# Channel mixing as 512 and 384 columns, and the last 64 keys' product as native float32

## The chip, the core and the metric

One core of a Trainium2 chip runs the whole program. The metric is the time of one execution on the device, in microseconds. Three runs of the kernel before took 436.41 to 436.9, with a median of 436.66.

## The reference

Three networks in a row, all in float32, on 2 batches of 448 tokens. First attention with 12 heads of 64, whose scores are capped by a tanh; then a gated network that mixes tokens; then a token and a channel mixing:

```python
scores = cap * np.tanh((q @ k.T) / sqrt(64) / cap)
attn = softmax(scores);  x = attn @ v                 # (2, 448, 768)
h = gelu(x @ w_in);  u, v = h[..., :512], h[..., 512:]
v_s = w_sg @ layer_norm(v) * g_ln + b_sg
x = x + (u * v_s) @ w_out
u = x + tokens(np.maximum(x.T @ w_tok1, 0) @ w_tok2)   # w_tok1 448x256
out = u + np.maximum(u @ w_ch1, 0) @ w_ch2             # w_ch1 768x1536
```

The change is in two places: `attn @ v` for the last 64 of the 448 keys, and the last line.

## The kernel before, in words

Activations lie as channels by tokens: 128 channels on the partitions, 448 tokens of one batch along the row. Nearly every product is done in three: an operand is split into a high part, rounded to the fp32r format, and a low part, the rest of it; high by high, high by low and low by high are added up in PSUM (`three`, `THREE`). The high part is a cast, the low part a subtraction, on whichever of ScalarE, VectorE and GpSimd the planner picks (`cast`, `rest`, `split`). Each 448-column product of this kind is one matmul, recorded at L276.

Attention runs over 12 pairs of heads (6 per batch). The 448 keys of a pair are three blocks of 128 and a remainder of 64. For the blocks, scores are fp32r products on 64 rows, one head on the lower and one on the upper half of TensorE (L545), then tanh and exp on ScalarE (L519, L527), then the product with the values in native float32 on 128 rows (L577), the operands unsplit. For the 64 remaining keys the two heads share one product on 128 rows (L660), tanh and exp give `tr`, and `tr` is split into `TH` and `TL`. The values of those keys come with the pair's queries and keys as 128 extra columns (`RC`) of the `qk` tensor, so they are split together with them (L353, L357 or L352, and L369). `rest_of` then adds their part to the two heads' outputs: three terms, each for the lower and the upper head, six fp32r products on 64 rows (L566). Normalising the pair follows on VectorE.

After attention come the gated network, token mixing (`tok1_unit`, `tok2_unit`) and channel mixing. `ch1_unit` makes one of 12 blocks of 128 hidden channels: 18 products of 448 columns for batch 0, 18 for batch 1, then a split ReLU. `ch2_unit` makes one of 6 blocks of output channels: 36 products for batch 0, 36 for batch 1, and adds the residual, which GpSimd sums up from its two parts beforehand (L911), on VectorE (L1031). Each batch has 6 tiles `x` of its own for these inputs, [128, 2, 448].

The order of all this is not that of the code. A planner (`Plan.schedule`) gives each operation a duration, due key and possible engines, and lists it on the engine where it can start first; buffers are handed out by due keys too, from the counts in `BUFS`. The emitted order is what every engine then follows.

Of the kernel before, what the change touches and what calls it, by code (L numbers as in the profile page):

```python
# [17 lines left out]
NP = H // 2  # L18
DM = H * D
ND = DM // 128  # L20
DF = 512
NF = DF // 128
ST = 112
NS = S // ST
NR = 3
# [7 lines left out]
KJ = (0, 576, 704, 832)  # L33
QC, RC = slice(128, 576), slice(960, 1088)
QKW = 1088
THREE = ((0, 0), (0, 1), (1, 0))
# [33 lines left out]
}  # L70
BUFS = {"x": 12, "v": 3, "q": 6, "a": 21, "r": 2, "t": 3, "h": 13, "p": 6, "gm": 4, "sc": 2, "sm": 4}
SLOT = 203.0
# [19 lines left out]


class Op:
    __slots__ = ("ways", "key", "seq", "deps", "bufs", "new", "eng", "fn", "start", "end", "nbytes", "nwait")


class Plan:
# [5 lines left out]
    def op(self, ways, key, r=(), w=(), nbytes=0):  # L104

        o = Op()
        o.ways, o.key, o.seq, o.nbytes = ways, key, len(self.ops), nbytes
        o.deps, o.new = [], []
        o.bufs = list(dict.fromkeys(list(r) + list(w)))
        for b in o.bufs:  # L110
            if b.users == 0 and b.ap is None:
                o.new.append(b)
            b.users += 1
            write = any(b is x for x in w)
            if write or b.psum:
                o.deps += b.last_writers + b.readers
                if write:
                    b.last_writers, b.readers = [o], []
                else:
                    b.readers = [o]  # L120
            else:
                o.deps += b.last_writers
                b.readers.append(o)
        o.deps = list(dict.fromkeys(o.deps))
        self.ops.append(o)
        return o

    def schedule(self):
# [13 lines left out]
        free = {t: [0.0] * n for t, n in BUFS.items()}  # L142
        for b in {b for o in ops for b in o.bufs if b.ap is not None and b.tag in free}:
            free[b.tag].pop()
# [78 lines left out]
class Net:  # L223
    def __init__(self, tc, io, pool, ps, anycap=False):
        self.tc, self.nc, self.io, self.pool, self.ps, self.anycap = tc, tc.nc, io, pool, ps, anycap
        self.plan = Plan()
        self.key = 0.0
        self.last_exp = None
        self.exps = {}
# [11 lines left out]
    def h(self, shape, dtype=F32):  # L241
        return self.buf("h", shape, dtype)

    def bank(self):
# [224 lines left out]
    def pair_in(self, n):  # L469
# [30 lines left out]
        def part(i, rows, cs):  # L500
# [3 lines left out]

        V = self.buf("v", [128, 9, 64])
        self.load(
            128 * 576 * 4,
            lambda: nc.sync.dma_start(out=V.ap.rearrange("p c d -> p (c d)"), in_=io["va"][b, p]),
# [25 lines left out]
    def scores(self, qk, js, key, more=(), extra=0.0):  # L534
# [5 lines left out]
        def fn():  # L540
# [10 lines left out]
        self.pe(  # L551
            3 * len(js) + 3 * len(more) + 0.5,
            fn,
# [5 lines left out]

    def rest_of(self, qk, T, A):  # L560
        part, tiles = qk[:2]
# [6 lines left out]
        return fn, [*tiles, *T], A  # L568

# [17 lines left out]
    def normalise(self, n, A):  # L587
# [30 lines left out]
        for h, rows in ((0, LO), (1, UP)):  # L618
# [9 lines left out]
            )  # L628
        x = self.buf("x", [128, 2, S], F32R)
        self.split(S, lambda: x[:, 0], lambda: x[:, 1], lambda: xf.ap, [xf], [x], kn, ON["XH"], ON["XL"])  # L630
        return x

    def attention_all(self):
# [3 lines left out]
        for n in range(B * NP + 1):  # L637
            k0 = 10.0 * n
            if n < B * NP:
                qk = self.pair_in(n)  # L640
                E = {j: self.a([128, 2, S]) for j in range(3)}
                tr, TH, TL = self.h([128, 1, S]), self.h([128, S], F32R), self.h([128, S], F32R)
                A = [self.bank() for _ in range(2)]
                for js in ([[0], [1]] if n == 0 else [[0, 1]]):
                    for i, (j, sc) in enumerate(zip(js, self.scores(qk, js, k0 + 0.3 * js[0]))):
                        self.weigh(sc, 2, E[j], k0 + 0.1 * j)
            if old:
                oqk, oE, oT, oA = old
                self.values(oqk, oE, oA, [0, 1], k0 + 0.5)
                more = [self.rest_of(oqk, oT, oA)]  # L650
            if n < B * NP:
# [4 lines left out]
                def last(sc=sc, part=qk[0]):  # L656
# [8 lines left out]
                self.rest(  # L665
                    S,
                    lambda TL=TL: TL.ap,
                    lambda tr=tr: tr[:, 0],
                    lambda TH=TH: TH.ap,
                    [tr, TH],  # L670
                    [TL],
                    k0 + 5,
                    ON["TL"],
                )
            else:
                f, r, w = more[0]
                self.pe(3.5, f, r, w, k0 + 4)
            if old:
                self.values(oqk, oE, oA, [2], k0 + 5)
                xs.append(self.normalise(n - 1, oA))  # L680
            if n < B * NP:
                old = qk, E, (TH, TL), A
        return xs

    def attention_anycap(self, n):
# [10 lines left out]
        for h, r in ((0, LO), (1, UP)):  # L696
            for m in range(NS):
# [68 lines left out]
                )  # L766
        x = self.buf("x", [128, 2, S], F32R)
        self.split(S, lambda: x[:, 0], lambda: x[:, 1], lambda: xf.ap, [xf], [x], k0 + 8)
# [213 lines left out]

    def tok2_unit(self, h1, w2, x2, d):
        nc = self.nc
# [7 lines left out]
        self.dve(S, lambda: nc.vector.tensor_tensor(out=z.ap, in0=ps[:, :S], in1=z.ap, op=ALU.add), [ps, z], [z])  # L992
        u = self.buf("x", [128, 2, S], F32R)
        self.split(S, lambda: u[:, 0], lambda: u[:, 1], lambda: z.ap, [z], [u])
# [3 lines left out]
    def ch1_unit(self, ws, U, f):  # L998
        ps = self.bank2()
        for b in range(B):  # L1000
            terms = []
            for d in range(ND):
                n, c = divmod(f % 2 * ND + d, 4)
                cs = slice(c * 128, (c + 1) * 128)
                terms += self.three(
                    lambda i, n=n, cs=cs: ws[n][:, i, cs], lambda i, d=d, b=b: U[b][d][:, i], [ws[n], U[b][d]]
                )
            self.mm(ps, lambda b=b: ps[:, b, :S], terms, 1)
        hi, lo = (self.buf("q" if f < 3 else "a", [128, 2, S], F32R) for _ in range(2))
        self.relu_split(2 * S, (hi, lambda: hi.ap), (lo, lambda: lo.ap), ps, lambda: ps[:, :, :S])  # L1010
        return [[hi, lo]] * B, lambda i, b: (hi, lo)[i][:, b]

    def ch2_unit(self, ws, h2, U, d):
        nc, io = self.nc, self.io
        for b in range(B):
            ps = self.bank()
            terms = []
            for f in range(NC):
                cs = slice(f % 4 * 128, (f % 4 + 1) * 128)
                terms += self.three(  # L1020
                    lambda i, f=f, cs=cs: ws[f // 4][:, i, cs], lambda i, f=f, b=b: h2[f][1](i, b), [ws[f // 4], *h2[f][0][b]]
                )
            self.mm(ps, lambda ps=ps: ps[:, :S], terms, 1)
            u = U[b][d]
            cuts = [slice(0, S // 2), slice(S // 2, S)] if (b, d) == (B - 1, ND - 1) else [slice(0, S)]
            o = [self.h([128, cs.stop - cs.start]) for cs in cuts]
            for i, cs in enumerate(cuts):
                self.whole(o[i], u, cs)
                self.dve(
                    cs.stop - cs.start,  # L1030
                    lambda o=o[i], ps=ps, cs=cs: nc.vector.tensor_tensor(out=o.ap, in0=ps[:, cs], in1=o.ap, op=ALU.add),  # L1031
                    [ps, o[i]],
                    [o[i]],
                )
            for i, (cs, out) in enumerate(zip(cuts, (nc.sync, nc.scalar))):
                self.load(
                    128 * (cs.stop - cs.start) * 4,
                    lambda o=o[i], b=b, cs=cs, out=out: out.dma_start(
                        out=io["out"][b, d * 128 : (d + 1) * 128, cs], in_=o.ap
                    ),  # L1040
                    [],
# [4 lines left out]
    def run(self):  # L1046
# [49 lines left out]
        for b in range(B):  # L1096
            U[b] = stage([lambda d=d: self.tok2_unit(h1[b], w2, x2[b], d) for d in range(ND)], 1.1)

# [40 lines left out]
def layout(q, k, v, cap, moe_w_in, moe_g_ln, moe_w_sg, moe_b_sg, moe_w_out,  # L1139
# [9 lines left out]
    qk = np.zeros((B, NP, 2, 64, QKW), q.dtype)  # L1149
    va = np.ones((B, NP, 128, 9, 64), v.dtype)  # L1150
    qk[..., RC] = 1.0
    for h in range(2):
# [5 lines left out]
        qk[:, :, h, :, QC] = q.reshape(B, NP, 2, S, D)[:, :, h].transpose(0, 1, 3, 2)  # L1158
        qk[:, :, h, :, RC.start + 64 * h : RC.start + 64 * h + 64] = vp[:, :, h, REST]
    return {  # L1160
        "qk": qk.reshape(B, NP, 128, QKW),
        "va": va.reshape(B, NP, 128, 576),
        "q": c(qt),
# [21 lines left out]
def build(arrays):  # L1185
# [6 lines left out]
    }  # L1192
    io["out"] = nc.dram_tensor("out_t", (B, DM, S), F32, kind="ExternalOutput").ap()
    with tile.TileContext(nc) as tc:
# [12 lines left out]
```

## Time and profile before

| | us |
|---|---|
| median of three runs | 436.66 |
| the profiled execution's own time | 437.02 |
| its span, first to last instruction | 435.1 |
| TensorE busy (2050 matmuls) | 424.8 |
| VectorE busy | 267.3 |
| ScalarE busy | 248.2 |
| GpSimd busy | 99.8 |

The busy time of an engine is an average over stages. Whether a stage is bound by it is read from the chain of waits, which goes back from the last instruction to what released each step. The granted TensorE clock is 1.00 in nearly all of the span. A native float32 product stands in the trace as two matmul records with a weight load each. A matmul's recorded duration is longer than its step, since products overlap; so steps are taken from starts, or from a run of many.

### The profile page before, as it was taken

The page shows a single profiled execution, that of the slowest core. Times are in us where ns is not written, and L with a number is a line of the kernel's source. Part 1 is how long each engine was busy: PE and PEld are TensorE (multiplying, and loading weights), DVE is VectorE, ACT ScalarE, POOL GpSimd, SP SyncE. Part 2 cuts the span into 40 slices and gives each one's busy share as a digit, 9 for nine tenths or more (in the row PEclk, how much of TensorE's full clock was granted, in tenths as well). Part 3 has the DMA queues.
Part 4 walks back from the last instruction along what each step waited for, and adds up shares of the span by engine and source line. Part 5 has one row for each costly group of instructions (what it writes and reads, how often), then busy time and mean ns, then how long its engine had stood idle before and what let it go on. Part 6 is the DMA issues. An engine that isn't in the chain of part 4 may idle for free.

```text
span 435.1 us, 5461 instructions
## 1 busy us (share of the span) xinstructions
PE 424.8 (98%) x2050; PEld 350.4 (81%) x2050; DVE 267.3 (61%) x422; ACT 248.2 (57%) x375; POOL 99.8 (23%) x100
## 2 busy tenths in 40 slices
PE   8997999999999999999999999999999999999994
PEld 5554556667676899999999999999999999999993
DVE  4799999887559966995567898665113233334210
ACT  5998899886858647527567717766223243253100
POOL 0343351121001321755023681201010011011100
PEclk9999999999999999999999999999999999999999
DMA  7535345464010302105302114544101232533010
GB/s 270 210 127 175 93 147 187 135 213 149 21 51 5 140 2 96 44 0 165 121 0 101 45 50 145 194 134 156 50 0 58 89 124 86 187 124 133 22 44 29
DMA packets 14866, 44.84 MB, mean 103 GB/s; under 512 B 1904, under 2 KB 4208, under 8 KB 14832
## 3 DMA queue, kind: packets, MB, share of 16 engines
q1 hardware_dynamic: 14688, 44.30, 30.5%
q8 instruction: 18, 0.29, 0.3%
q14 instruction: 16, 0.13, 0.1%
q10 hardware_dynamic: 144, 0.11, 0.1%
HBM read 41.65 MB, written 2.75 MB: 102 GB/s over the span
## 4 chain that ended last, share of the span: by engine, by line
PE 90%; DVE 6%; ACT 3%; issue 1%; POOL 0%; DVEq 0%; POOLq 0%
PE gm L276 52%; PE sc L276 21%; PE gm L577 9%; PE sc L545 4%; PE gm L566 1%; DVE t L454 1%; PE sc L660 1%; DVE q L369 1%; ACT a L519 1%; PE sc L925 1%; ACT a L527 1%; DVE t L443 1%; PE sc L344 1%; DVE h L621 1%; DVE h L597 0%
## 5 line engine op out<-in xcount | busy, mean ns | idle before, releaser
L276 PE MATMUL gm<-a,a 128*128 128x448 f32 (+1 forms) x556 | 115.2, 363 | 0.0
L276 PEld LDWEIGHTS gm<-a,a 128*128 128x128 f32 x556 | 102.8, 188 | 8.4
L276 PE MATMUL sc<-x,a 128*128 128x448 f32 x432 | 89.4, 368 | 0.0
L276 PEld LDWEIGHTS sc<-x,a 128*128 128x128 f32 x432 | 81.1, 188 | 8.2
L577 PE MATMUL gm<-a,v 128*128 128x448 f32 x144 | 60.6, 553 | 1.6 <-ACT a L527 1.6
L276 PE MATMUL gm<-q,a 128*128 128x448 f32 x268 | 57.3, 367 | 0.0
L432 DVE SCALAR_TENSOR_TENSOR t<-r,t 128x512 int32<-128x512 int32 (+1 forms) x52 | 39.7, 766 | 28.0 <-ACT t L425 28.0
L412 ACT ACTIVATE t<-r 128x512 uint16<-128x512 uint16 (+1 forms) x52 | 40.8, 784 | 24.8 <-DVE a L369 20.5
L276 PEld LDWEIGHTS gm<-q,a 128*128 128x128 f32 x268 | 50.3, 188 | 4.7
L401 ACT ACTIVATE r<-r 128x512 f32<-128x512 f32 (+1 forms) x58 | 38.9, 671 | 24.8 <-DMA r<-ch_in 22.2
L577 PEld LDWEIGHTS gm<-a,v 128*128 128x128 f32 x144 | 25.7, 189 | 25.2 <-issue 20.0
L370 POOL TENSOR_TENSOR a<-t,a 128x512 fp32r<-128x512 f32 x19 | 25.8, 1359 | 77.7 <-DVE a L353 59.0
L425 ACT ACTIVATE t<-r 128x512 f16<-128x512 f32 (+1 forms) x52 | 40.2, 774 | 0.0
L369 DVE TENSOR_TENSOR a<-t,a 128x512 fp32r<-128x512 f32 x37 | 26.0, 706 | 21.6 <-POOL a L357 20.1
L357 POOL TENSOR_SCALAR a<-t 128x512 fp32r<-128x512 f32 x18 | 11.1, 619 | 119.7 <-PE gm L276 72.0
L519 ACT ACTIVATE a<-sc,qs 128x896 f32<-128x896 f32 x36 | 35.0, 1004 | 5.3 <-PE sc L545 5.3
L527 ACT ACTIVATE a<-a,acap 128x896 f32<-128x896 f32 x36 | 36.5, 1043 | 0.1
L911 POOL TENSOR_TENSOR h<-x 128x448 f32<-128x448 f32 (+1 forms) x25 | 32.9, 1340 | 11.3 <-PE gm L276 6.1
L276 PE MATMUL gm<-x,a 128*128 128x448 f32 x144 | 31.4, 373 | 0.0
L958 DVE SCALAR_TENSOR_TENSOR a<-sc,a 128x896 fp32r<-128x896 f32 x9 | 9.8, 1092 | 34.3 <-ACT a L955 34.3
L276 PEld LDWEIGHTS gm<-x,a 128*128 128x128 f32 x144 | 27.0, 188 | 3.6 <-issue 1.4
L955 ACT ACTIVATE a<-sc 128x896 fp32r<-128x896 f32 x9 | 8.3, 918 | 33.8 <-PE sc L276 33.8
(102 smaller groups left out, 476.5 us busy)
## 6 DMA issues: line engine op xcount, KB each, us to landing
r<-ch_in SPq DMA_DIRECT2D x36, 512.0 KB, 3.3
r<-w_in_in SPq DMA_DIRECT2D x12, 512.0 KB, 4.1
q<-qk_in SPq DMA_DIRECT2D x11, 544.0 KB, 4.7
v<-va_in SPq DMA_DIRECT2D x12, 288.0 KB, 4.0
r<-w_out_in SPq DMA_DIRECT2D x6, 512.0 KB, 3.5
out_t<-h SPq DMA_DIRECT2D x11, 224.0 KB, 2.0
r<-tok_in SPq DMA_DIRECT2D x2, 512.0 KB, 3.4
t<-w_sg_in SPq DMA_DIRECT2D x4, 224.0 KB, 5.8
```

The lines of the kernel that those rows point to most:

```text
L276: self.nc.tensor.matmul(view(), l, rr, start=(i + m == 0), stop=(i + m == n - 1))
L369: "DVE": ("DVE", n / 0.96 + 155, lambda: nc.vector.tensor_tensor(**args()), not psum),
L370: "POOL": ("POOL", n * 2.3 + 60, lambda: nc.gpsimd.tensor_tensor(**args()), True),
L401: lambda: nc.scalar.activation(raw[:, :, 1].bitcast(F32), raw[:, :, 1].bitcast(F32), AF.Copy, scale=2.0**-112),
L412: lambda: nc.scalar.activation(t.ap.bitcast(U16)[:, 0::2], raw.ap.rearrange("p n t -> p (n t)").bitcast(U16)[:, 1::4], AF.Copy, scale=2.0* ...
L425: lambda: nc.scalar.activation(t.ap.bitcast(F16)[:, 1::2], raw[:, :, 1].bitcast(F32), AF.Copy),
L432: lambda: nc.vector.scalar_tensor_tensor(out=t.ap, in0=raw[:, :, 1], scalar=3, in1=t.ap, op0=ALU.logical_shift_left, op1=ALU.bitwise_or),
L519: lambda: nc.scalar.activation(te.ap, sc[:, 0:nn, :S], AF.Tanh, scale=self.qs),
L527: lambda: nc.scalar.activation(te.ap, te.ap, AF.Exp, scale=self.acap),
L545: nc.tensor.matmul(sc[:, h, :S], part(k, rows, ks), part(q, rows, QC), start=(t == 0), stop=(t == 2))
L577: nc.tensor.matmul(A[h][:, :S], V[:, 3 * j + h : 3 * j + h + 2].rearrange("p c d -> p (c d)"), E[j][:, h], start=(j == 0), stop=(j == 2),)
L911: lambda: self.nc.gpsimd.tensor_tensor(out=out.ap, in0=parts(0), in1=parts(1), op=ALU.add),
```

## The change

For the last 64 keys: `tr` is no longer split. `rest_of` now makes two native float32 products on 64 rows, one per head, with the unsplit `E[3]` and with the values' columns moved from `qk` (1088 to 960 columns) to the tensor `va` (576 to 704). The cast `TH` and the subtraction `TL` of each pair go. The planner's duration for `rest_of` grows from 3 to 3.7 slots.

For channel mixing: the two batches' 896 tokens lie side by side in one tile per channel block (`Part` gives each batch its half, and `x` has 6 tiles of double width), and the products run over tokens 0 to 511 and 512 to 895 instead of over the batches. The output tensor is laid out as (768, 896).

```diff
+WIDE = slice(0, 512), slice(512, 2 * S)
-QC, RC = slice(128, 576), slice(960, 1088)
-QKW = 1088
+QC = slice(128, 576)
+QKW = 960
-BUFS = {"x": 12, "v": 3, "q": 6, "a": 21, ...
+BUFS = {"x": 6, "v": 3, "q": 6, "a": 21, ...
+class Part(Buf):
+    def __init__(self, whole, cs):
+        self.whole, self.cs, self.tag, self.psum = whole, cs, None, False
...
+    @property
+    def ap(self):
+        return self.whole.ap[:, :, self.cs]
...
+    def x_part(self, d, b):
+        if b == 0:
+            self.both[d] = self.buf("x", [128, 2, B * S], F32R)
+        return Part(self.both[d], slice(b * S, (b + 1) * S))
...
-        V = self.buf("v", [128, 9, 64])
+        V = self.buf("v", [128, 11, 64])
...
-            for v, e in THREE:
-                for h, rows in enumerate((LO, UP)):
-                    self.nc.tensor.matmul(A[h][:, :S], part(v, rows, RC), T[e][rows], start=False, stop=False)
+            for h, rows in enumerate((LO, UP)):
+                self.nc.tensor.matmul(
+                    A[h][:, :S],
+                    qk[2][rows, 9:11].rearrange("p c d -> p (c d)"),
+                    E[3][rows, 0],
+                    start=False,
+                    stop=False,
+                )
...
-                self.weigh(sc, 1, tr, k0 + 4.1)
-                self.cast(S, lambda TH=TH: TH.ap, lambda tr=tr: tr[:, 0], [tr], [TH], k0 + 5, ON["TH"])
-                self.rest(
...
+                self.weigh(sc, 1, E[3], k0 + 4.1)
...
     def ch1_unit(self, ws, U, f):
         ps = self.bank2()
-        for b in range(B):
+        for m, ts in enumerate(WIDE):
...
-                    lambda i, n=n, cs=cs: ws[n][:, i, cs], lambda i, d=d, b=b: U[b][d][:, i], [ws[n], U[b][d]]
-                )
-            self.mm(ps, lambda b=b: ps[:, b, :S], terms, 1)
+                    lambda i, n=n, cs=cs: ws[n][:, i, cs],
+                    lambda i, d=d, ts=ts: U[0][d].whole[:, i, ts],
+                    [ws[n], U[0][d], U[1][d]],
+                )
+            size = ts.stop - ts.start
+            self.mm(ps, lambda m=m, size=size: ps[:, m, :size], terms, size / S)
...
     def ch2_unit(self, ws, h2, U, d):
-        for b in range(B):
+        for m, ts in enumerate(WIDE):
...
-            self.mm(ps, lambda ps=ps: ps[:, :S], terms, 1)
+            self.mm(ps, lambda ps=ps, size=size: ps[:, :size], terms, size / S)
```

Three places of the order show what moves. The first is TensorE in the second step of the third pair: its third block of scores (`sc_283`), the remainder of the second pair (`gm_228` and `gm_237` are that pair's two heads, `h_263` and `h_273` its `TH` and `TL`, `q_148` and `q_154` the split values), and the last block's values. Before:

```order
L545 MATMUL sc_283<-q_213 128x448 x2
L545 MATMUL sc_283<-q_218,q_213 128x448 x2
L545 MATMUL sc_283<-q_213,q_218 128x448 x2
L566 MATMUL gm_228<-h_263,q_148 128x448
L566 MATMUL gm_237<-h_263,q_148 128x448
L566 MATMUL gm_228<-h_273,q_148 128x448
L566 MATMUL gm_237<-h_273,q_148 128x448
L566 MATMUL gm_228<-h_263,q_154 128x448
L566 MATMUL gm_237<-h_263,q_154 128x448
L577 MATMUL gm_228<-a_222,v_95 128x448
```

Six products stand between the scores and the values. The same place of the change (`sc_268` the scores, `h_229` the unsplit weights, `v_95` the values, L594 is `rest_of`, L694 the remainder's scores, L611 the values):

```order
L574 MATMUL sc_268<-q_186 128x448 x2
L574 MATMUL sc_268<-q_201,q_186 128x448 x2
L574 MATMUL sc_268<-q_186,q_201 128x448 x2
L594 MATMUL gm_225<-h_229,v_95 128x448
L594 MATMUL gm_233<-h_229,v_95 128x448
L694 MATMUL sc_286<-q_186 128x448
L694 MATMUL sc_286<-q_201,q_186 128x448
L694 MATMUL sc_286<-q_186,q_201 128x448
L611 MATMUL gm_225<-a_214,v_95 128x448
```

Two products are left, first one head's and then the other's, and a product on 128 rows follows them. The second place is TensorE's entry to channel mixing. Before (`sc_2426` and `sc_2483` are the first two units, `x_2302` to `x_2372` the six tiles of batch 0, `x_2382` to `x_2435` those of batch 1):

```order
L276 MATMUL sc_2426<-x_2372,a_2185 128x448 x3
L276 MATMUL sc_2426<-x_2382,a_2165 128x448 x3
L276 MATMUL sc_2426<-x_2405,a_2165 128x448 x3
L276 MATMUL sc_2426<-x_2410,a_2165 128x448 x3
L276 MATMUL sc_2426<-x_2420,a_2165 128x448 x3
L276 MATMUL sc_2426<-x_2424,a_2185 128x448 x3
L276 MATMUL sc_2426<-x_2435,a_2185 128x448 x3
L276 MATMUL sc_2483<-x_2302,a_2185 128x448 x3
```

Batch 1 is first read after 18 products. In the change `x_2200` to `x_2263` are the six tiles of both batches, `sc_2313` and `sc_2335` the first two units:

```order
L305 MATMUL sc_2313<-x_2200,a_2063 128x512 x3
L305 MATMUL sc_2313<-x_2215,a_2063 128x512 x3
L305 MATMUL sc_2313<-x_2227,a_2063 128x512 x3
L305 MATMUL sc_2313<-x_2238,a_2063 128x512 x3
L305 MATMUL sc_2335<-x_2200,a_2083 128x512 x3
L305 MATMUL sc_2335<-x_2215,a_2083 128x512 x3
L305 MATMUL sc_2335<-x_2227,a_2108 128x512 x3
L305 MATMUL sc_2335<-x_2238,a_2108 128x512 x3
L305 MATMUL sc_2313<-x_2251,a_2083 128x512 x3
L305 MATMUL sc_2313<-x_2263,a_2083 128x512 x3
L305 MATMUL sc_2313<-x_2200,a_2063 128x384 x3
```

Twelve products of the second unit have moved ahead of the first unit's last two tiles. The third place is VectorE just before it (L369 and L992 before, L398 and L1015 after): the sums with the residual, and the splits' low parts. Before, the end of batch 1:

```order
L992 TENSOR_TENSOR h_1885<-gm_2374,h_1885 128x448
L992 TENSOR_TENSOR h_1901<-gm_2386,h_1901 128x448
L992 TENSOR_TENSOR h_1915<-gm_2397,h_1915 128x448
L992 TENSOR_TENSOR h_1934<-gm_2412,h_1934 128x448
L369 TENSOR_TENSOR x_2405<-h_1861,x_2405 128x448
L369 TENSOR_TENSOR x_2410<-h_1885,x_2410 128x448
L369 TENSOR_TENSOR x_2420<-h_1901,x_2420 128x448
L369 TENSOR_TENSOR x_2424<-h_1915,x_2424 128x448
L369 TENSOR_TENSOR x_2435<-h_1934,x_2435 128x448
```

All sums stand ahead of the last five low parts. The same of the change:

```order
L398 TENSOR_TENSOR x_2215<-h_1764,x_2215 128x448
L398 TENSOR_TENSOR x_2227<-h_1788,x_2227 128x448
L398 TENSOR_TENSOR x_2238<-h_1799,x_2238 128x448
L1015 TENSOR_TENSOR h_1811<-gm_2292,h_1811 128x448
L1015 TENSOR_TENSOR h_1826<-gm_2304,h_1826 128x448
L398 TENSOR_TENSOR x_2251<-h_1811,x_2251 128x448
L398 TENSOR_TENSOR x_2263<-h_1826,x_2263 128x448
```

The last two sums have moved in between the low parts.

## Rows read from the trace of the kernel before

**Rows 1.** The page: busy us of each engine (share of the span).

```profile
PE 424.8 (98%) x2050; PEld 350.4 (81%) x2050; DVE 267.3 (61%) x422; ACT 248.2 (57%) x375; POOL 99.8 (23%) x100
```

**Rows 2.** Chain of waits in order of time: start us, us, what.

```profile
37.80 1.21 DVE q L369
...
39.03 1.10 ACT q L352
...
43.16 0.99 PE gm L577 x2
...
129.15 0.61 PE gm L566 x6
...
130.56 4.51 PE gm L577 x12
...
250.49 89.28 PE sc L276 x432
339.77 89.29 PE gm L276 x432
```

**Rows 3.** Timeline of TensorE, 36 to 46 us: start us, us, engine, line, what.

```profile
37.44 0.48 PE L545 MATMUL sc<-q 64*128 64x448 f32 x2
39.06 0.67 PE L545 MATMUL sc<-q,q 64*128 64x448 f32 x4 [1.14 <-DVE q L369]
...
41.40 0.57 PE L660 MATMUL sc<-q,q 128*128 128x448 f32 x2
43.16 0.99 PE L577 MATMUL gm<-a,v 128*128 128x448 f32 x2 [1.19 <-ACT a L527]
```

**Rows 4.** Timeline of TensorE around one pair's remainder.

```profile
128.99 0.77 PE L566 MATMUL gm<-h,q 64*128 64x448 f32 x6
129.69 0.47 PE L660 MATMUL sc<-q 128*128 128x448 f32 x1
130.00 0.56 PE L660 MATMUL sc<-q,q 128*128 128x448 f32 x2
```

**Rows 5.** Timeline of TensorE by width; then by-form groups (busy us, mean ns).

```profile
149.67 4.24 PE L276 MATMUL gm<-a,p 128*128 128x512 f32 x18
153.75 14.76 PE L276 MATMUL gm<-x,a 128*128 128x448 f32 x72
168.34 18.00 PE L276 MATMUL gm<-q,a 128*128 128x448 f32 x88
...
225.75 9.52 PE L276 MATMUL gm<-a,a 128*128 128x384 f32 x54
...
L276 PE MATMUL gm<-a,a 128*128 128x384 f32 x88 | 16.2, 338 | 0.0
...
L276 PEld LDWEIGHTS sc<-x,a 128*128 128x128 f32 x432 | 81.1, 188 | 8.2
```

**Rows 6.** Groups in the first 45 us (busy us, mean ns), then timelines of VectorE and GpSimd.

```profile
L370 POOL TENSOR_TENSOR h<-h,h 128x448 fp32r<-128x448 f32 x3 | 3.4, 1136 | 2.9 <-ACT h L352 2.9
L352 ACT CAST h<-h 128x448 fp32r<-128x448 f32 x3 | 1.8, 586 | 0.0
L369 DVE TENSOR_TENSOR h<-h,h 128x448 fp32r<-128x448 f32 x1 | 0.6, 618 | 0.0
...
21.63 1.37 DVE L454 SCALAR_TENSOR_TENSOR t<-r,t 128x512 int32<-128x512 int32 x1
24.23 0.69 DVE L454 SCALAR_TENSOR_TENSOR t<-r,t 128x512 int32<-128x512 int32 x1
37.72 1.28 DVE L369 TENSOR_TENSOR q<-q,q 128x1088 fp32r<-128x1088 f32 x1
...
21.33 1.13 POOL L370 TENSOR_TENSOR h<-h,h 128x448 fp32r<-128x448 f32 x1 [0.99 <-ACT h L352]
```

**Rows 7.** Timelines of VectorE and GpSimd at the entry to channel mixing.

```profile
251.07 5.63 DVE L369 TENSOR_TENSOR x<-h,x 128x448 fp32r<-128x448 f32 x5
...
251.76 10.70 POOL L911 TENSOR_TENSOR h<-x 128x448 f32<-128x448 f32 x8 [1.77 <-DVE x L369]
```

More of the change, by code (lines that the diff above doesn't have):

```diff
@@ L109, in op @@
         o.bufs = list(dict.fromkeys(list(r) + list(w)))
-        for b in o.bufs:
-            if b.users == 0 and b.ap is None:
+        held = []
+        for b in list(o.bufs):
+            if isinstance(b, Part):
+                held.append(b.whole)
+            elif b.users == 0 and b.ap is None:
                 o.new.append(b)
@@ L123, in op @@
                 b.readers.append(o)
+        for b in dict.fromkeys(held):
+            if b.users == 0:
+                o.new.append(b)
+            b.users += 1
+            o.bufs.append(b)
         o.deps = list(dict.fromkeys(o.deps))
@@ L142, in schedule @@
         free = {t: [0.0] * n for t, n in BUFS.items()}
-        for b in {b for o in ops for b in o.bufs if b.ap is not None and b.tag in free}:
+        for b in {b for o in ops for b in o.bufs if b.tag in free and b.ap is not None}:
             free[b.tag].pop()
@@ L227, in __init__ @@
         self.key = 0.0
+        self.both = {}
         self.last_exp = None
@@ L551, in scores @@
         self.pe(
-            3 * len(js) + 3 * len(more) + 0.5,
+            3 * len(js) + 3.7 * len(more) + 0.5,
             fn,
@@ L558, in scores, with rest_of @@
         return scs
-    def rest_of(self, qk, T, A):
-        part, tiles = qk[:2]
+    def rest_of(self, qk, E, A):
         def fn():
-            for v, e in THREE:
-                for h, rows in enumerate((LO, UP)):
-                    self.nc.tensor.matmul(A[h][:, :S], part(v, rows, RC), T[e][rows], start=False, stop=False)
-        return fn, [*tiles, *T], A
+            for h, rows in enumerate((LO, UP)):
[6 more added lines that the diff above has]
+                )
+        return fn, [qk[2], E[3]], A
     def values(self, qk, E, A, js, key):
@@ L647, in attention_all @@
             if old:
-                oqk, oE, oT, oA = old
+                oqk, oE, oA = old
                 self.values(oqk, oE, oA, [0, 1], k0 + 0.5)
-                more = [self.rest_of(oqk, oT, oA)]
+                more = [self.rest_of(oqk, oE, oA)]
             if n < B * NP:
@@ L681, in attention_all @@
             if n < B * NP:
-                old = qk, E, (TH, TL), A
+                old = qk, E, A
         return xs
@@ L1035, in ch2_unit @@
             for i, (cs, out) in enumerate(zip(cuts, (nc.sync, nc.scalar))):
+                at = slice(ts.start + cs.start, ts.start + cs.stop)
                 self.load(
[L1037 to L1040, printed above, removed]
+                    128 * size // n * 4,
+                    lambda o=o[i], at=at, out=out: out.dma_start(out=io["out"][d * 128 : (d + 1) * 128, at], in_=o.ap),
                     [],
@@ L1096, in run @@
         for b in range(B):
-            U[b] = stage([lambda d=d: self.tok2_unit(h1[b], w2, x2[b], d) for d in range(ND)], 1.1)
+            U[b] = stage([lambda d=d: self.tok2_unit(b, h1[b], w2, x2[b], d) for d in range(ND)], 1.1)
         c1 = {}
@@ L1149, in layout @@
     qk = np.zeros((B, NP, 2, 64, QKW), q.dtype)
-    va = np.ones((B, NP, 128, 9, 64), v.dtype)
-    qk[..., RC] = 1.0
+    va = np.ones((B, NP, 128, 11, 64), v.dtype)
     for h in range(2):
@@ L1192, in build @@
     }
-    io["out"] = nc.dram_tensor("out_t", (B, DM, S), F32, kind="ExternalOutput").ap()
+    io["out"] = nc.dram_tensor("out_t", (DM, B * S), F32, kind="ExternalOutput").ap()
     with tile.TileContext(nc) as tc:
```

58 lines of the change are left out of this document (30 added, 28 removed).

## Prediction

> **What bounds the kernel now.** I read the page's first block first: TensorE is busy 424.8 of 435.1 us and no other engine above 61% [rows 1]. The chain of waits then says where that matters. Until 43.16 us it runs mainly through VectorE and ScalarE; from there to 429.06 it is TensorE without a gap, and 178.57 us of it are the two channel stages, 864 products in two unbroken pieces [rows 2]. So after 43 us every change of TensorE's time counts in full and relief of another engine counts nothing; before, TensorE waits for VectorE's lateness at two places, which its timeline shows [rows 3]. Third come the steps of single products: in attention [rows 4], and by width [rows 5]. Two tables end the reading: what VectorE, ScalarE and GpSimd do for the last 64 keys in the first 45 us [rows 6], and the entry to channel mixing [rows 7].
>
> **The rest of the keys, product itself.** Removed per pair of heads are six fp32r products on 64 rows. They stand on the chain with 0.61 us [rows 2]: upper and lower half run together, three steps of 0.203. Added are two native products. A native product leaves two records in the trace; twelve records on 128 rows take 4.51 us [rows 2], 0.376 each, so there are four records of 0.376 where six of 0.203 went by twos. No row shows native products on 64 rows. Bounds: two steps, if the heads share as the fp32r ones do (0.75); four, if they share nothing (1.50). The nearest rows are L566's: there the program alternates the halves, and only neighbours in program order run together. In the new code the first head's two records come first and the second head's two behind. In that order record 2 has to wait for record 1 (same rows), record 3 can go beside record 2, record 4 waits for 3: three steps, 1.13 us. I take that: 0.52 more per pair, 12 pairs, +6.2 us (bounds +1.7 and +10.7). What follows each time is a product on 128 rows, so the second head's last record has nothing beside it. In the first pair TensorE still waits for ScalarE, so I take off 0.3.
>
> The Trainium skill (TensorE: Matmul & The Clock Gate, The mechanism) states that products start and end strictly in program order and only weight loads are pulled ahead; it speaks against this part, since by it the cheap bound can't be had. The starts in [rows 4] agree, but show nothing on native records. By it the sum is the one below; were it not so here, the first rival's.
>
> **Around it.** A change between 64 and 128 rows costs some 0.19: from the rest's start to the next product's it is 0.70 instead of 0.61, and that first product takes 0.31 to the next instead of 0.207 [rows 4]. The order has 48 such changes before and 46 after: -0.4.
>
> Removed from the other engines per pair are a cast (0.59 on ScalarE, or on GpSimd) and a subtraction (1.14 on GpSimd, 0.62 on VectorE), and the split of queries and keys shrinks from 1088 to 960 columns (0.15 less of an undisturbed 1.28) [rows 2, 6]. After 43 us all this lies beside TensorE and is worth nothing. Before, it is. At 37.44 TensorE wants the fifth pair's scores and goes on only at 39.06, since VectorE's split of that pair ends at 39.01; at 41.40 it has to wait until 43.16 for ScalarE, which had itself waited for that split until 39.03 [rows 2, 3]. Less the ordinary steps (0.20 and 0.41) these are 1.42 and 1.35, together 2.77 us. Up to there VectorE loses one subtraction (0.6), five smaller splits (0.8) and, where GpSimd's subtraction ran beside it, a stretch (1.37 for an operation of 0.69, while GpSimd's 1.13 ran) [rows 6]. That is 1.4 to 2.1 us; 1.6 is needed, and TensorE itself comes to the place three rests, 1.6 us, later. Both waits should go: -2.8. If they stay or another takes their place, the sum loses what they cost. The queue of loads has the same 832 KB per pair (64 KB go from one tensor to the other) in nearly the same order; I price it at nothing, since the loads before the first scores get shorter, not longer, and from 43 us on no wait for them is on the chain; were one late, ScalarE's wait rather than TensorE's would show it first.
>
> **Channel mixing.** Terms and weights stay; 864 products of 448 columns become 432 of 512 and 432 of 384. In the stages themselves the step at 448 is 89.28 / 432 = 0.2067 [rows 2]. At 512 columns 18 products go from start 149.67 to the next run's at 153.75: 0.2267. At 384 it is 54 in 9.52, from which the last one's own duration of 0.34 comes off: 53 steps of 0.1732 [rows 5]. A pair of 448 costs 0.4133, of 512 and 384 0.3999: 13.4 ns, by 432 gives -5.8 us. The gain is there because 448 lies above the line between its neighbours (0.1999); what does that I can't read. In other stretches 448 runs at 14.59 / 72 = 0.2026 [rows 5]; if the 4 ns belong to the stage and not to the width, the new widths pay them too and the gain falls to 13.4 - 8 = 5.4 ns, -2.3 us. That is the near bound; the far one is nothing at all (third rival). I take -5.8, since both new widths have shown one step throughout. Weight loads of 188 ns [rows 5] did not keep 384 columns from steps of 173.
>
> The price is the entry. So far the first 18 products read batch 0 alone; now the first 512 columns need batch 1 at once. The planner answers by putting the second unit's first twelve products in between: the last two tiles of batch 1 are wanted 24 and 27 products after the start, at +5.4 and +6.1 us, where before it was +6.2 and +6.8. VectorE's last five splits ended at 256.70, 6.2 after the start at 250.49 (5.63 for five, slowed by GpSimd, which added tiles up beside them) [rows 2, 7]. If it does no better, the last tile is some 0.1 late; if the two sums now placed between them cost some 0.4 each there, 0.9; nothing, if GpSimd starts its sums later, as its order says. I take +0.3. A stage 3% shorter asks for its weights 3% sooner; the chain has no gap in either mixing stage now [rows 2], and both preparing engines have time left over the whole span [rows 1], so I price that at nothing; if one weight tile were late it would cost a fraction of its own conversion. The tail's halves shrink from 224 to 192 columns: under 0.1, left out.
>
> **Sum**: +6.2 - 0.3 - 0.4 - 2.8 - 5.8 + 0.3 = -2.8 us. The profiled execution took 437.02 (span 435.1 and 1.9 around it), so 434.2; the median of the runs shown is 0.36 lower, so **433.9**.
>
> **Rivals.** (a) The heads share the native products fully: two steps, +1.7 instead of +6.2. For it: the fp32r halves do, two products per 0.203. Against it: the order of the records. Sum -7.3, **429.4**. (b) They share nothing: four steps of 0.376, a rest of 1.50, +10.7. For it: no native product on 64 rows has been seen to share. Against it: the fp32r halves of the same height and columns do share [rows 4]. The place is the end of every pair, twelve times, all but the first few on the chain and those few in TensorE's own order; from a rest of 1.36 us on (the other terms are -9.0, by 12 is 0.75) the kernel is slower than before. Sum +1.7, **438.4**. (c) Uneven widths bring nothing: a step is a fixed part and a part by column, so 512 and 384 cost what two 448 do. Against it: the three steps of [rows 5] do not lie on a line. Were the excess all the stage's, the mixing would stay at 178.6 and the sum would be +3.0, 439.7. The Trainium skill has this rule (TensorE: Matmul & The Clock Gate, Back-to-back issue gap: in ns, the columns by 2.4 and 2.5 more); by it both pairs take 378 ns, an estimate from that page; the trace has 413 for the pair of 448, so it does not agree at this width. (d) The new order is late somewhere that the old one was not: the entry to mixing by its 0.9, or the first 43 us by their 2.8; forecast or a little above, 434.5 to 437.
>
> **How the numbers follow.** Forecast 0.55, with its own range 432.5 to 435.3 (entry, waits, and a step that differs by stage); (a) 0.16; (b) 0.16; (c) 0.05; (d) 0.08. A measurement of this kernel tells 0.2% (0.9 us) from no change: the three runs lie 0.5 apart. Faster, below 435.8: nearly all of the forecast, (a) and half of (d): 0.71. Slower, above 437.5: (b) mostly and (c): 0.19. The same: 0.10. The range from 429.1 to 438.8 leaves out (c) and about a third of (a) and of (b).
>
> **What would show it.** After: the rest's two products take 1.1 us from their first start to the next product's (0.75 or 1.5 for the rivals), with the first and second head's records overlapping once. The chain turns to TensorE well before 43 us and TensorE waits nowhere over 0.5 us between 30 and 45. The mixing's two stages together last 172.8 instead of 178.6, with steps of 0.227 and 0.173; a step of 0.181 at 384 or 0.231 at 512 would be the stage's share. At the entry TensorE stands still under 1 us. Wrong above all: a rest over 1.36 us.

## The result and the profile after

The changed kernel takes 431.58 us (median of 4, 431.17 to 432.13) against 436.78 for the kernel before on the same chip: ratio 0.9882, 95% interval 0.9865 to 0.9899, or 5.2 us less. The forecast was 433.9. The profiled execution took 431.57 us, span 429.8.

The page of the changed kernel, busy time of each engine, answers to [rows 1]:

```profile
PE 420.9 (98%) x2026; PEld 342.5 (80%) x2026; DVE 259.0 (60%) x417; ACT 244.0 (57%) x366; POOL 87.0 (20%) x90
```

The chain of waits (start us, us, what) answers to [rows 2]:

```profile
40.87 0.75 PE gm L594 x4
...
47.78 1.02 ACT a L548
...
127.61 0.75 PE gm L594 x4
...
129.17 4.51 PE gm L611 x12
...
136.33 65.82 PE gm L305 x316
...
249.27 87.17 PE sc L305 x432
336.45 86.82 PE gm L305 x432
```

Three things are to be seen. The remainder, two native products and four records (L594), takes 0.75 us, two steps of 0.375, where 0.61 stood before. The two mixing stages take 173.99 us instead of 178.57. And between 14.6 us and the last product a single tanh at 47.78 is the chain's only piece on another engine, where before VectorE and ScalarE held it until 43.16.

The chain's piece at the end of attention, before:

```profile
137.56 65.80 PE gm L276 x316
```

| us | before | after | difference |
|---|---|---|---|
| start to the end of attention (start of the piece x316) | 137.56 | 136.33 | -1.23 |
| token stages, with the entry to mixing | 112.93 | 112.94 | 0.0 |
| the two mixing stages | 178.57 | 173.99 | -4.58 |
| last product to the end of the span | 6.1 | 6.5 | +0.4 |

TensorE's timeline (start us, us, engine, line, what) around one remainder answers to [rows 4]:

```profile
82.59 0.47 PE L574 MATMUL sc<-q 64*128 64x448 f32 x2
82.90 0.56 PE L574 MATMUL sc<-q,q 64*128 64x448 f32 x4
83.30 0.91 PE L594 MATMUL gm<-h,v 64*128 64x448 f32 x4
84.14 0.47 PE L694 MATMUL sc<-q 128*128 128x448 f32 x1
84.45 0.57 PE L694 MATMUL sc<-q,q 128*128 128x448 f32 x2
```

From the remainder's first start to the next product's it is 0.84 us, 0.14 more than the 0.70 of before. In the single starts, two records begin 3 ns apart, two more 375 ns later, again 3 ns apart. The same view between 36 and 50 us answers to [rows 3]:

```profile
36.87 0.47 PE L574 MATMUL sc<-q 64*128 64x448 f32 x2
37.18 0.57 PE L574 MATMUL sc<-q,q 64*128 64x448 f32 x4
...
41.86 0.57 PE L694 MATMUL sc<-q,q 128*128 128x448 f32 x2
42.26 4.67 PE L611 MATMUL gm<-a,v 128*128 128x448 f32 x12
...
47.78 0.57 PE L574 MATMUL sc<-q,q 64*128 64x448 f32 x4
48.85 0.47 PE L574 MATMUL sc<-q 64*128 64x448 f32 x2 [0.49 <-ACT a L548]
```

The two waits of before are gone. One is new: from 47.78 to 48.85 are 1.07 us instead of an ordinary 0.41, so 0.66. All twelve records of the values stand ahead of these scores, so three score tiles follow each other, and the third needs the bank that the tanh at 47.78 frees.

In the mixing stages the steps at 512 and 384 columns are 226.7 and 173.3 ns, but not at once. These are the differences of neighbouring starts, in ns, from a change of width on, in one run of each width in the first stage:

```
512: 230 233 236 224 231 236 228 232 231 227 226 227 227 226 227 227 226 227
384: 171 175 177 185 176 182 173 174 173 173 174 173 173 174 173 173 174 173
```

A change to 512 columns costs 41 ns over the even steps, one to 384 costs 26 (4 in one place, where the run of 512 before it had only six products). The 35 changes make 1.13 us, and the first run of 512, behind products of another kind, 0.05 more: nearly the whole distance of 1.19 from 173.99 to the forecast's 172.8.

### The profile page after: what moved, and what is told of

Read it like the earlier page. It is cut to its first block, busy times and chain, and to the rows that moved or that the text cites. A ratio compares the mean times of both kernels' runs of the same rounds, so it can differ in the third digit from the quotient of the medians.

```text
span 429.8 us, 5380 instructions
## 1 busy us (share of the span) xinstructions
PE 420.9 (98%) x2026; PEld 342.5 (80%) x2026; DVE 259.0 (60%) x417; ACT 244.0 (57%) x366; POOL 87.0 (20%) x90
## 4 chain that ended last, share of the span: by engine, by line
PE 96%; ACT 2%; issue 0%; POOL 0%; DVE 0%; DVEq 0%; POOLq 0%
PE gm L305 52%; PE sc L305 20%; PE gm L611 12%; PE sc L574 6%; PE gm L594 2%; PE sc L694 2%; ACT a L548 1%; PE sc L948 1%; PE sc L373 1%; ACT a L556 1%; ACT h L556 0%; ACT r L430 0%; ACT h L548 0%; DVE h L1066 0%; POOL ident masks.py:199 0%
## 5 line engine op out<-in xcount | busy, mean ns | idle before, releaser
L305 PE MATMUL gm<-a,a 128*128 128x384 f32 (+2 forms) x556 | 113.1, 359 | 0.0
L305 PEld LDWEIGHTS gm<-a,a 128*128 128x128 f32 x556 | 100.6, 188 | 8.6
L305 PE MATMUL sc<-x,a 128*128 128x512 f32 (+1 forms) x432 | 87.3, 363 | 0.0
L305 PEld LDWEIGHTS sc<-x,a 128*128 128x128 f32 x432 | 78.3, 188 | 8.9
L611 PE MATMUL gm<-a,v 128*128 128x448 f32 x144 | 59.7, 548 | 0.4 <-ACT a L556 0.4
L305 PE MATMUL gm<-q,a 128*128 128x448 f32 (+2 forms) x268 | 57.0, 366 | 0.0
L399 POOL TENSOR_TENSOR a<-t,a 128x512 fp32r<-128x512 f32 x18 | 24.5, 1362 | 118.7 <-DVE a L382 105.0
L611 PEld LDWEIGHTS gm<-a,v 128*128 128x128 f32 x144 | 26.2, 189 | 22.7 <-issue 19.5
L398 DVE TENSOR_TENSOR a<-t,a 128x512 fp32r<-128x512 f32 x38 | 29.2, 770 | 19.6 <-POOL a L386 18.7
L548 ACT ACTIVATE a<-sc,qs 128x896 f32<-128x896 f32 x36 | 35.0, 1004 | 7.8 <-PE sc L574 7.6
L305 PE MATMUL gm<-a,x 128*128 128x512 f32 x108 | 26.5, 401 | 0.0
```

The lines of the kernel that those rows point to most:

```text
L305: self.nc.tensor.matmul(view(), l, rr, start=(i + m == 0), stop=(i + m == n - 1))
L398: "DVE": ("DVE", n / 0.96 + 155, lambda: nc.vector.tensor_tensor(**args()), not psum),
L399: "POOL": ("POOL", n * 2.3 + 60, lambda: nc.gpsimd.tensor_tensor(**args()), True),
L548: lambda: nc.scalar.activation(te.ap, sc[:, 0:nn, :S], AF.Tanh, scale=self.qs),
L611: nc.tensor.matmul(A[h][:, :S], V[:, 3 * j + h : 3 * j + h + 2].rearrange("p c d -> p (c d)"), E[j][:, h], start=(j == 0), stop=(j == 2),)
```

## The experiments

Theory: (1) the heads share the native products fully, because a record on one half of the rows may pass records that wait for the other half; (2) the lighter VectorE took TensorE's early waits away; (3) mixing gains by width and loses at each change of width. Rivals stand in the expectations. Each run has executions of the kernel before on its own chip beside it; their medians lie between 436.65 and 436.92 us, so times from two different runs are compared to no better than 0.3 us.

**Mixing alone** (mix_alone): the changed kernel with the remainder and its split of before.

```diff
-                    qk[2][rows, 9:11].rearrange("p c d -> p (c d)"),
-                    E[3][rows, 0],
...
+            for v, e in THREE:
+                for h, rows in enumerate((LO, UP)):
+                    self.nc.tensor.matmul(A[h][:, :S], part(v, rows, RC), T[e][rows], start=False, stop=False)
```

> The attention of before (the last keys' product as three fp32r products a head), with only the channel mixing of the change: joined tiles, 512 and 384 columns. If the two parts of the change act apart from each other, the attention ends where it does in before (TensorE's chain up to 137.6 us), the two mixing stages take 174.0 us together as in the changed kernel (178.6 before) and the tail keeps its 0.5 us: some 4.1 us under before. Rival: the gain belongs to the new instruction order as a whole, and the attention moves too: the chain then leaves 137.6 us by over 0.5 us, and the sum with the other part run alone is not the 5.2 us of both together.

432.29 us, ratio to before 0.9897 (0.9882 to 0.9913): 4.4 less. The chain:

```profile
137.41 65.80 PE gm L305 x316
...
250.34 87.17 PE sc L305 x432
337.51 86.82 PE gm L305 x432
```

Attention ends within 0.15 us of before, and the stages are the changed kernel's to 0.01 us. Mixing's gain does not hang on the rest of the change. TensorE's two early waits stand here as before (1.1 us for VectorE, then 1.2 for ScalarE): they hang on the part that is left out.

**The remainder alone** (rest_alone): 448 and 448 columns on the joined tiles.

```diff
-WIDE = slice(0, 512), slice(512, 2 * S)
+WIDE = slice(0, S), slice(S, 2 * S)
```

> The whole change but with 448 and 448 columns in the channel mixing on the joined tiles: the native product and its order alone. By the two-step reading of the trace (1.7 us more products, the 2.8 us of VectorE-caused waits gone, one new wait of 0.7 us): 1.2 us under before, the chain at 136.3 us instead of 137.6, and the mixing stages at 178.6 us with steps of 206.7 ns and no longer steps after a change of tokens. Rival: the longer steps (up to 185 and 236 ns) that the changed kernel shows at the start of each run of one width come from the joined tile and not from the change of width: then some steps of 215 ns stand here too and the stages take 179.8 us.

435.18 us, 0.9964 (0.995 to 0.9978): 1.5 less. The chain, from its first long piece:

```profile
1.63 3.88 DMA cap<-cap_in
...
6.49 2.61 PE sc L574 x12
...
137.06 65.82 PE gm L305 x316
...
250.01 89.28 PE sc L305 x432
339.29 89.29 PE gm L305 x432
```

The stages are as long as before, and every step in them is 206 or 207 ns: the joined tile is not what makes steps longer. The two early waits are gone here, and TensorE's only wait after 10 us is one of 0.5. This profiled execution started its scores late, behind the load of the cap; so the end of attention, 137.06, is not to be compared to 0.5 us, and that this part brings more than 1 us rests on the median. The parts alone make 5.8 us, together 5.2; the intervals, 0.6 to 0.7 us to either side of each, leave that difference open.

**Turned order of widths** (turn_about): 20 changes of width instead of 35 (the expectation counted some 18).

```diff
-        for m, ts in enumerate(WIDE):
+        for m, ts in list(enumerate(WIDE))[:: 1 if f % 2 else -1]:
```

(In the second stage the same with `d`.)

> The changed kernel with the two widths in turned order in every second unit (512, 384, then 384, 512), so that the width changes some 18 times in the two stages instead of 36. If each change of width costs the 35 ns that the eight steps behind it show in the trace of the changed kernel: 0.6 us less, and the stages take 173.4 us instead of 174.0. Rival: the longer steps belong to the start of each group of products into a new bank of PSUM, whatever its width: then every second run still shows them in its middle, and the time is the changed kernel's within 0.2 us.

431.10 us, 0.9872 (0.9857 to 0.9887). The chain:

```profile
249.23 86.87 PE sc L305 x432
336.10 86.62 PE gm L305 x432
```

173.49 us, 0.50 less for 15 changes fewer, 33 ns each. In a run of one width the steps in the middle, where a new bank begins, are no longer than the others. So the extra belongs to the change of width. The medians, 0.48 apart, agree, though the two ranges overlap.

**Heads apart** (heads_apart): the score tiles' products head by head.

```diff
-                for t, (k, q) in enumerate(THREE):
-                    for h, rows in enumerate((LO, UP)):
+                for h, rows in enumerate((LO, UP)):
+                    for t, (k, q) in enumerate(THREE):
```

> The changed kernel with the three products of a score tile issued head by head (three on the lower 64 rows, then three on the upper) and not in turn; 36 such tiles. If TensorE starts its records strictly in the order of the program, only the third of the lower head has the first of the upper beside it: five steps of 0.2 us instead of three, 0.4 us more for each tile, 14 us in all (446 us), wherever TensorE is the bound. If a record on one half of the rows may pass one that waits for the other half, three steps remain and the time is the changed kernel's within 1 us. This tells why the two-record native product of the heads takes two steps: in the second case by passing, in the first because its records already come in turn.

431.96 us, 0.4 over the changed kernel, not 14. TensorE's timeline around the same remainder as above:

```profile
82.89 0.48 PE L574 MATMUL sc<-q 64*128 64x448 f32 x2
83.20 0.57 PE L574 MATMUL sc<-q,q 64*128 64x448 f32 x4
83.60 0.92 PE L594 MATMUL gm<-h,v 64*128 64x448 f32 x4
```

The six products still take 0.71 us. In the starts the upper head's first record begins 10 ns behind the lower's, not behind its third; 10 ns for 36 tiles is 0.36 us; the two ranges of times overlap, so the 0.4 rests on the starts. The compiled program lists the lower head's three products first, as the code does, so the records pass on the chip. The Trainium skill (TensorE: Matmul & The Clock Gate, The mechanism) has matmuls strictly in program order; here the trace does not agree, and the measurement decides.

**Six and six** (heads_far): in eleven pairs the first two tiles' products as six lower, then six upper.

```diff
-            for sc, j in zip(scs, js):
+            for h, rows in enumerate((LO, UP)):
+                for sc, j in zip(scs, js):
...
```

> The changed kernel with the first two score tiles of each of eleven pairs issued as six products on the lower 64 rows, then six on the upper (the other score tiles three and three). If a record may pass any number of records that wait for the other half, these two tiles still take six steps, with the upper head some 20 ns behind the lower: within 0.7 us of the changed kernel. If TensorE can only look past a few, the upper head starts when the lower has that few left, each of the eleven places is longer by at least one step (0.2 us), and the time is over 2 us longer; the step at which the upper head starts tells how far it looks.

437.02 us (one execution), 5.4 over the changed kernel. Its timeline at one such place, and its chain there:

```profile
81.15 0.47 PE L574 MATMUL sc<-q 64*128 64x448 f32 x1
81.46 0.57 PE L574 MATMUL sc<-q,q 64*128 64x448 f32 x2
81.67 0.56 PE L574 MATMUL sc<-q 64*128 64x448 f32 x2
```

```profile
81.22 1.93 PE sc L574 x12
83.15 3.20 PE gm L611 x8
```

1.93 us instead of 1.42. The lower head starts three products alone. The last line is the upper's first product, at 81.67, and the lower's fourth, 0.2 us behind it. When the upper starts, the lower's third has just begun (6 ns earlier) and three still wait; it is so in all eleven places. Passing has a limit. The lower's fourth product carries a wait for its bank, so this run by itself cannot tell a limit of three records from a stop at that wait; the next one can.

**The remainder doubled** (rest_double).

```diff
-            for h, rows in enumerate((LO, UP)):
+            for h, rows in ((0, LO), (0, LO), (1, UP), (1, UP)):
```

> The changed kernel with the last keys' product issued twice for each head, first both of the lower head, then both of the upper: eight records, and the output adds these keys twice. If the upper head's records may pass the four of the lower head that stand before them (nothing among them waits for a semaphore), the eight take four steps of 0.375 us, 1.5 us instead of 0.75 in the chain, and 12 of them add at most 9 us (some 8 to 9 us in all, 439.5 to 440.5). If TensorE starts records strictly in order, only one of the upper's has a lower beside it: seven steps, 2.6 us, 22 us more. If it looks past only three records, five steps: 1.9 us, 13.5 us more.

441.75 us (one execution). The chain and the timeline around one:

```profile
88.45 0.80 PE sc L574 x6
89.25 1.61 PE gm L594 x8
90.86 0.81 PE sc L694 x3
```

```profile
89.09 1.77 PE L594 MATMUL gm<-h,v 64*128 64x448 f32 x8
90.79 0.47 PE L694 MATMUL sc<-q 128*128 128x448 f32 x1
```

Eight records take 1.61 us: four steps and 0.11, not 1.9 or 2.6. The upper head's first record begins 6 ns behind the lower's first, past three that wait; its later ones run 0.11 behind. Twelve times 0.86 more is 10.3; measured, 10.2, a little over the 9 expected, for those 0.11. Native records pass as fp32r ones do. The weight loads show how far. In the changed kernel, where two records of the lower head stand ahead, both heads' first weights are loaded within 10 ns of each other, some 0.2 us before the first record starts. Here, where four stand ahead, only the lower's are; the upper's first load begins 4 ns behind the start of the lower's first record, when three are left waiting. Both hold in eleven of the twelve pairs, where no record among these waits for a semaphore; in the last pair the first load itself waits for one. So three are passed and four are not, and the stop in heads_far needs no wait to explain it.

**The split kept** (split_kept): the two tiles are made as before; nothing reads them.

```diff
+                TH, TL = self.h([128, S], F32R), self.h([128, S], F32R)
...
+                self.cast(S, lambda TH=TH: TH.ap, lambda tr=E[3]: tr[:, 0], [E[3]], [TH], k0 + 5, ON["TH"])
+                self.rest(
...
```

> The changed kernel in which the weights of the last 64 keys are still split into two fp32r tiles by VectorE, GpSimd or ScalarE, as before; nothing reads these tiles. If TensorE's 2.8 us of waits near 37 and 41 us went because this split (and VectorE's share of it) went, waits of over 1 us that end at VectorE come back before 60 us and the time rises by 1 to 2.8 us over the changed kernel's 431.6 (to 432.6 to 434.4). Rival: they went with the narrower q and k tiles or with the new instruction order, and the time stays within 0.4 us.

432.67 us, 1.1 over the changed kernel. TensorE's waits from 14 to 140 us (engine, line waited for: us in total, times, longest; the changed kernel has only the wait for L548 there, once, 0.5 us), then the chain:

```profile
PE sc L574 <- ACT a L548: 1.0, 2, 0.5
PE gm L305 <- DVE h L655: 0.7, 1, 0.7
PE sc L574 <- DVE q L398: 0.2, 1, 0.2
```

```profile
54.53 1.06 DVE q L398
55.59 1.55 DVE t L483
...
60.52 1.14 DVE q L398
61.69 0.63 DVE h L655
...
137.84 65.82 PE gm L305 x316
```

The chain runs through VectorE until after 61 us, and attention ends 1.5 us later, in an execution that was 0.5 over its median. The split's work, with the order that the planner makes for it, is worth 1.1 to 1.5 us, at the low end of what was expected. The sign that was expected did not come: no wait of over 0.7 us came back at one place, the loss is spread.

**Wider tiles** (q_wide): `QKW = 1056` for 960.

> The changed kernel with tiles of 1056 instead of 960 columns for keys and queries (before had 1088): three quarters of the removed columns are loaded and split again, and nothing reads them. VectorE's part of a tile (1.28 us at 1088 columns in before) grows by some 0.11 us and its transfer by a tenth. If the narrower tiles took the two waits away: 1 to 2.8 us over the changed kernel's 431.6. If the split of the last weights did, as predicted: within 0.4 us of it.

431.86 us, 0.3 over the changed kernel, and attention ends at 136.60 us, 0.27 later; one wait of 0.4 us for VectorE's split of queries and keys appears. By the times alone the 0.3 is not told from nothing, since the two ranges overlap. The narrower tiles are the small part, if any.

**Six cuts** (widths), second stage.

```diff
-        for m, ts in enumerate(WIDE):
+        cut = (512, 504, 496, 480, 464, 456)[d]
+        for m, ts in enumerate((slice(0, cut), slice(cut, 2 * S))):
```

> The changed kernel with another cut of the 896 tokens for each of the six blocks of the second mixing stage: 512/384, 504/392, 496/400, 480/416, 464/432 and 456/440. The trace so far has the step at 512 and 384 columns as columns/2.4 plus 13.3 ns and at 448 as columns/2.4 plus 20.0 ns. Theory one: every width that is not a multiple of 128 has the 20: steps of 220.0 at 480 columns, 193.3 at 416, 226.7 at 496 and 186.7 at 400, and the stage is 2.3 us longer than the 86.8 us of the changed kernel (6.7 ns times 360 products less the 72 of the first block). Theory two: 448 is a bad width by itself and the others have 13.3: 213.3 at 480, 186.7 at 416, 220.0 at 496, and the stage is within 0.4 us of 86.8.

431.93 us (one execution). Mean steps from starts, after the first 12 products of each run; 448 is from rest_alone. Columns/2.4 is a yardstick: the ns that one column per cycle would take at 2.4 GHz, the level that the granted clock of 1.00 stands for.

| columns | 512 | 504 | 496 | 480 | 464 | 456 | 448 | 440 | 432 | 416 | 400 | 392 | 384 |
|---|---|---|---|---|---|---|---|---|---|---|---|---|---|
| step, ns | 226.7 | 226.7 | 223.3 | 216.7 | 208.9 | 208.9 | 206.7 | 200.1 | 195.8 | 186.7 | 180.0 | 178.3 | 173.3 |
| over columns/2.4 | 13.3 | 16.7 | 16.7 | 16.7 | 15.5 | 18.9 | 20.0 | 16.8 | 15.8 | 13.3 | 13.3 | 15.0 | 13.3 |

The stage took 87.40 us against 86.82. Neither theory holds: the part over columns/2.4 takes several values between 13.3 and 20.0, with 448 the worst of thirteen widths, and 512, 416, 400 and 384 the best. Of the six cuts none is better than 512 and 384. What sets the steps stays open. The width alone does not: 448 columns, 206.7 here, run at 202.7 in the 244 products of the token stages that follow a run of 512 without a gap, in before as in the changed kernel. The new widths were each seen behind one neighbour only. Nor does every change cost what one between 512 and 384 does: over the first 12 products, those between the other widths here came to between -28 and +18 ns.

**Values behind the scores** (turn_behind): the turned order, and the values of the second 128 keys stand behind the next pair's first scores.

```diff
-                self.pe(3.7, av, [V, E[j]], [A[h]], key)
+                o = self.pe(3.7, av, [V, E[j]], [A[h]], key)
+                if j == 1 and behind:
+                    o.deps.append(behind)
...
```

(`behind` is the operation of the next pair's first scores.)

> The kernel with the turned order of widths, and in the written order the values of the second 128 keys always stand behind the first scores of the next pair, as they do already for most pairs. In the changed kernel one pair has all its values ahead of these scores, and TensorE then waits 0.66 us at 48 us for ScalarE's tanh to free a bank. If that wait comes from the missing products between the second and the third score tile, it goes, and the time falls from 431.1 to some 430.5. Rival: TensorE then waits about as long at these scores for VectorE's split of the keys (a wait for q in place of the wait for the bank), and the time stays within 0.2 us of 431.1 or rises.

430.63 us (430.47 to 431.34), 0.9861 of before (0.9845 to 0.9878): the lowest median of the case, some 0.9 us under the changed kernel. The chain at the place, and the end of attention:

```profile
42.35 3.01 PE gm L611 x8
45.35 1.53 PE sc L574 x12
46.89 1.70 PE gm L611 x4
48.59 0.81 PE sc L574 x6
...
135.99 65.82 PE gm L305 x316
```

The wait for the bank is gone, and 0.1 us is left at the scores. Attention ends only 0.3 us earlier than in turn_about, the medians differ by 0.47; a third of a microsecond is what the trace shows. The rest of the 0.66 went into the order: by the starts, the products change between 64 and 128 rows 48 times here and 46 times in turn_about, and two such changes at the prediction's 0.19 are 0.38. Putting the values behind the scores ends the wait and costs these two.

## Why the prediction was right and where it was wrong

Faster was right, by more than forecast: -5.2 us instead of -2.8. The 431.58 lies under the forecast's own range of 432.5 to 435.3, about midway to the first rival's 429.4. The direction owes something to luck: with the three steps forecast for the remainder, the same kernel would have gained some 0.7 us, less than the 0.9 that the prediction tells from no change. It came out clearly faster because the largest term was wrong in its favour.

- **The remainder: wrong.** The failed step is "In that order record 2 has to wait for record 1 (same rows), record 3 can go beside record 2, record 4 waits for 3: three steps". The upper head's records do not wait for their turn: two steps, +0.14 us each, +1.7 us in all instead of +6.2. The row behind it showed alternating halves running in pairs; that only neighbours in program order can do so was read into it, and heads_apart refutes it. This term alone is 4.5 us.
- **The early waits: gone, as forecast** (-2.8); mix_alone keeps them and rest_alone does not have them. But one new wait took 0.66 back, the kind of rival (d), from the same rebuilt order that saves two changes between 64 and 128 rows: +1.7 - 0.3 - 0.4 - 2.8 + 0.66 is -1.1, and attention gave -1.23. The -0.3 for the first pair, sized for the longer remainder, was not measured by itself. The cause was priced too simply: the split returned alone costs 1.1 to 1.5 and the narrower tiles some 0.3; what is left of the 2.8 is not told apart from the order, and split and wider tiles were not run together. The condition that TensorE arrive 1.6 us later was not needed: it came to the place at 36.87, 0.57 earlier than before.
- **Mixing: the mechanism right, the size off.** The even steps are those read from [rows 5], and 4.58 of 5.8 us came. The missing 1.2 are the 35 changes of width, which the forecast priced at nothing; the rows showed only long runs of one width. The 4 ns by which 448 is slower here are no toll of the stage, as the near bound had it, since the new widths run in it at the steps that they have elsewhere. They do not belong to the width alone either, since 448 has two steps in one trace; why it has them stays open. (By the 4 ns, the sign at 384 columns would have been a step of 0.177, not 0.181.)
- **The entry**: +0.3 forecast, 0.0 measured. **The tail**: left out of the forecast, +0.4 measured. From the last product to the end of the span it is 6.1 and 6.2 us in the two kernels with 448 and 448 columns (before and rest_alone) and 6.3 to 7.0 in the other ten, one trace each; so it goes with the uneven widths or the new cut of the output, and why is not shown. The last transfers do not tell it: they took 4.0 us to land in the changed kernel and 2.7 at most in heads_apart, with the same tail of 6.5.

From forecast to result: -4.5 (remainder) + 0.7 (new wait) + 1.2 (changes of width) - 0.3 (entry) + 0.4 (tail) = -2.5 us; the distance is 2.4.

## What to carry to other kernels

Count products on half the rows per half: the longer half sets the time, even where the program lists one half behind the other, as long as no more than three records must be passed. Read the step of each width from a trace before cutting a dimension, in the stage where it is to run (448 columns had two steps here), and keep runs of one width long, turning the order at each unit. When an instruction order is rebuilt, look for the wait that it makes as well as for those it removes.

## What the runs showed of the hardware

- A record on 64 rows starts while up to three records of the other half that stand ahead of it wait (rest_double, 6 ns behind). With more ahead, its weights were loaded only when three were left (rest_double from four, heads_far from six).
- A native float32 record on 64 rows takes the same 0.375 us as one on 128 rows, and two heads share it fully.
- A change to 512 columns behind a run of 384 costs 41 ns over its first nine products, one to 384 behind a long run of 512 costs 26; between other widths no fixed cost was seen (widths, -28 to +18 ns).
- Steps are not a straight line in columns: 504 columns cost as much as 512 (226.7 ns), 456 as much as 464 (208.9). And 448 has two: 202.7 in one stretch of 244 products, 206.7 in the others.
